# Gated attention with a low-rank mixer: order of loads around slot 7, PSUM tiles of the first pairs, whole-block squares in the first batch, cover in the short slots

## The chip, the cores and the metric

The kernel runs on one core of one Trainium2 chip. The metric is device microseconds of one execution, the median of several runs. The core has TensorE (PE) for matmuls, VectorE (DVE) and ScalarE (ACT) for elementwise work, GpSimd (POOL), and SyncE (SP), whose queue issues nearly all the DMA transfers of this kernel, one after the other.

## The reference

```python
def _attn_ref(u, v, z):                       # u, v: 8 x 3136 x 256, z: 8 x 3136 x 64
    scale = 1.0 / S
    scores = scale * np.matmul(z, z.transpose(0, 2, 1))
    attn = np.maximum(scores, 0.0) ** 2
    return u * np.matmul(attn, v)

def _moe_ref(x, U, V, w_ch1, w_ch2):          # U: 3136 x 32, V: 32 x 3136, w: 256 x 1024, 1024 x 256
    h = x.transpose(0, 2, 1) @ U @ V
    u = x + h.transpose(0, 2, 1)
    ch = np.maximum(u @ w_ch1, 0.0) @ w_ch2
    return u + ch
```

For each of eight batches: scores of z with itself, a squared relu, the product with v, a gate by u (this gives x), a rank-32 mix along the sequence (this gives x + h), and a two-layer channel mix with a residual. Inputs and output are float32; the kernel works in bfloat16 inside.

## The kernel before

**Tiling.** The 3136 rows of a batch are cut into NG = 7 groups: six of 512 rows (g = 0 to 5) and a short one of 64 rows (g = 6, called NQ). The scores are symmetric, so a block of 512 x 512 scores is computed once (two pairs of matmuls, 1024 columns each) and turned by a transposing DMA for its mirror image (`issue_turn`, line 416). Blocks are bfloat16 tiles `blk0` to `blk19`; scores and all other matmul results pass through four PSUM tiles `ps0` to `ps3` (`take_ps`, line 148). A block on the diagonal is made in a split layout (`score_finish_split`), with a turn of its own, the split turn. The product of scores and v is called AV.

**From score to block.** `rectify` (line 366) turns the PSUM result of a pair into bfloat16 by a relu on ACT or DVE, and `square` (line 362) squares it in place on DVE: line 364 in the profile. `score_finish` (line 491) does this for each pair on its own, so that each half of a block (1024 columns) has its own square, held until the planner thinks that its relu is done. In slot 0 the first pairs are handled by a list, `ways`: the first two, called "half", are split between ACT (lines 376, 380) and DVE (lines 377, 381), each engine taking one of the two 512-column banks of the same PSUM tile.

**Slots.** The work goes through 56 slots, t = 0 to 55, one for each item (b, g), in the loop from line 1347. Slot t holds the AV of item t; from t = 7 on x + h of item t - 7 (`u2_unit`, line 823: the rank-32 part, the sum, and the transposing DMA that gives the tile u2T, line 785); and from t = 8 on the channel mix of item t - 8 (`ch1_part`, line 922, which reads u2T and w1, then `ch2_stream`, line 1010, which reads w2). The score pairs of later items, `todo[t]`, are laid in between as cover: PE has them to do while other work waits. The slots with g = 6 (t = 6, 13, 20, ...) are the short ones: the AV of 64 rows is `av_small` (line 703, 50 matmuls), and the order of the parts is the list `order` (line 1439). The scores of the short group are turned by a DMA into `last_sb` (`last_turn`, line 551).

**What sets the order.** The schedule is written out by the program (`manual_schedule`). A planner clock (`clock[0]`) advances by the matmuls that are issued, in units of 256 columns, and `book` keeps estimated times for ACT, DVE and SP. `hold(due, f)` (line 121) puts work off until the planner clock reaches `due`; `emit` (line 1110) merges a stream of AV matmuls with queues of other parts, each with its place in the stream. On the chip each engine runs its instructions in the order in which they were issued, and waits by semaphore.

**First loads.** In the first slots weights are loaded between other work: `first_loads` (line 1232) gives U in slot 2, V in slots 3 and 4, w1 in slot 5 and w2 in slot 6 (`load_w`, line 1183, two halves). In slots 0 to 7 each load step is held at `clock + 5 + 22 * i` (line 1379), and the next group's u (`load_u`, line 304) at `clock + 60` (line 1381). In slot 7 (batch 1, g = 0) the z of the next batch is loaded in two pieces, the second with small transfers for the tail rows of z and v. Casts of what a slot loaded are held in the next slot (line 1365). In slot 7 x + h is done for the first time, and slot 8 holds the first channel mix.

Of the kernel before, what the change touches and what calls it, by code (L numbers as in the profile page):

```python
# [18 lines left out]
def kernel(  # L19
# [11 lines left out]
    nc = tc.nc  # L31
# [70 lines left out]
    ready_turns = []  # L102
    urgent = []
    slot = [0]
    ways = ["half", "half", "both", "dve"]
    waiting = [0]

    def needed(e):
# [12 lines left out]
    def hold(due, f):  # L121
        held.append((due, len(held), f))
# [243 lines left out]
    def rectify(dst, src, b, part=1, whole=False):  # L366

        ready = clock[0] + 3
        dve, act = max(free_at["dve"], ready), max(free_at["act"], ready)
        if whole and slot[0] == 0:  # L370
            dve += 6.5 * waiting[0]
            ends = {"dve": dve + DVE, "act": act + 19, "both": max(act + 8.7, dve) + 7.5}
            given = bool(ways)
            way = ways.pop(0) if ways else min(ends, key=lambda w: ends[w])
            if way == "half":
                nc.scalar.activation(out=dst[:, 0], in_=src[:, 0], func=AF.Relu, scale=scale)
                nc.vector.tensor_scalar(  # L377
                    out=dst[:, 1], in0=src[:, 1], scalar1=scale, scalar2=0.0, op0=ALU.mult, op1=ALU.max
                )
                nc.scalar.activation(out=dst[:, 0], in_=dst[:, 0], func=AF.Square)  # L380
                nc.vector.tensor_tensor(out=dst[:, 1], in0=dst[:, 1], in1=dst[:, 1], op=ALU.mult)  # L381
                done = max(book("act", ready, 5.2), book("dve", ready, 6.2))
                return done, max(book("act", ready, 5.2), book("dve", ready, 3.5))
            if way == "dve":
                if not given:
                    run_held(ready + 9)
                return one_pass(dst, src, ready)
            if way == "act":
                nc.scalar.activation(out=dst, in_=src, func=AF.Relu, scale=scale)
                nc.scalar.activation(out=dst, in_=dst, func=AF.Square)  # L390
                done = book("act", ready, 8.7)
                book("act", ready, 8.7)
                return done, free_at["act"]
        elif dve + 8 * part < act:
            nc.vector.tensor_scalar(  # L395
                out=dst, in0=src, scalar1=scale, scalar2=0.0, op0=ALU.mult, op1=ALU.max
            )
            return book("dve", ready, 11.2 if part == 1 else 6.4), None
        nc.scalar.activation(out=dst, in_=src, func=AF.Relu, scale=scale)  # L399
        return book("act", ready, 8.7 if part == 1 else 5.3), None  # L400
# [36 lines left out]
    def score_pairs(jobs):  # L437
# [50 lines left out]
            )  # L488
        return made

    def score_finish(made):
        for dst, k, ps, turn, key in made:
            if key and split(*key):
                score_finish_split(dst, k, ps, turn, key)
                continue
            if turn:
                J, g, b = turn
                unturned[blocks[b, g, J][0]] = False
            done, whole = rectify(dst, ps, key[0] if key else 0, whole=True)
            ps_free[k] = done  # L500
            waiting[0] += whole is None

            def finish(dst=dst, turn=turn, key=key, whole=whole):
                if whole is None:
                    waiting[0] -= 1
                    square(dst)
                if key:
                    squared[key] = squared.get(key, 0) + 1
                if turn:
                    hold(clock[0] + (7 if whole is None else 1), lambda: ready_turns.append(turn))  # L510

            hold(whole or done, finish)

    def score_finish_split(flat, k, ps, h, key):
# [23 lines left out]
    def score_burst(jobs):  # L538
        score_finish(score_pairs(jobs))


    def place_of(jt):

# [662 lines left out]
    def load_V(i0):  # L1206
# [27 lines left out]
        3: lambda: load_V(0),  # L1234
        4: lambda: load_V(2),
        5: lambda: load_w(0),
        6: lambda: load_w(1),
    }


# [70 lines left out]
    clock[0] = 43  # L1311
    free_at.update(dve=46, act=47)
    jobs0 = jobs_of(0, 0)
    score_burst(jobs0[:1])
    score_burst(jobs0[1:2])
    score_burst(jobs0[2:3])
    clock[0] = 60

# [1 line left out]
    for b in range(B):  # L1320
        for g in range(NQ):
            t = b * NG + g - 1
            new = jobs_of(b, g)
            if g == 0 and b > 0:
                x, y = (5, 10) if b == 1 else (5, 11)
                todo[t - 2] += new[:x]
                todo[t - 1] += new[x:y]
                todo[t] += new[y:12] if b == 1 else new[y:]
                todo[t + 1] += new[12:] if b == 1 else []
            elif b == 0 and g == 0:  # L1330
                todo[0] += new[3:]
            elif b == 0 and g and g % 2 == 0:
                todo[t] += new[:-1]
                todo[t + 1] += new[-1:]
            else:
                todo[t] += new
# [5 lines left out]
    direct = (B - 1, 0)  # L1342

    def early(b, g):
        return b > 1 and g == NQ

    for t in range(n_items):
        slot[0] = t
# [9 lines left out]
            load_u(*items[t + 1])  # L1358
        if t > NG and g_now == NQ and b_next < B:
            hold(clock[0] + 60 + 70, lambda b=b_next: load_u(b, NQ))  # L1360
        if t == n_items - 3:
            xTs[direct] = take_block()[1][:, : GT // 2, :].rearrange("p a (q d c) -> p (a q) d c", d=ND, c=P)
            x_turn(*direct, xTs[direct])
        for i, f in enumerate(casts_next):
            hold(clock[0] + (90 if g_now == NQ and b_next > 1 else 60 if t == NG else 15 if t >= NQ else 45) + 12 * i, f)
        casts_next = []
        spare += spare_next
        spare_next.clear()
        steps = load_part(b_next, g_now) if b_next < B else []
        steps += first_loads[t]() if t in first_loads else []  # L1370

        def load(step):
            casts_next.extend(step())
# [1 line left out]
        for i, f in enumerate(steps):  # L1375
            if t > NG:
                load(f)
            else:
                hold(clock[0] + 5 + 22 * i, lambda f=f: load(f))
        if t <= NG:  # L1380
            hold(clock[0] + 60, lambda t=t: load_u(*items[t + 1]))
        if g_now == 0 and t:
            last_turn(att[0])
        if b_next < B and g_now == 2:
# [24 lines left out]
        if av and full:  # L1409

            last = nA - 9
            for h, x, y in zip(hs, (4, 22, 36, 62), (16, 32, 48, last)):
                qc.append((x, 1, False, one(h, 0)))
                qc.append((y, 0 if y == 32 else 1, y != 32, lambda h=h, y=y: (scores(y != 32), one(h, 1)())))
            n = len(mine) - 3
            qs += [(9 + 74 * i / n, 1, False, lambda: scores(1)) for i in range(n)]
        elif av:

            if mix:
                qc += [(x, 1 - way, False, lambda way=way: ch1_small(*mix, way, box1)) for way, x in ((0, 36), (1, 48))]  # L1420
            if fin:
                qc.append((72, 2, False, lambda: (ch2_small(*fin), av_small(att[0], NQ))))
            k = min(2, len(mine) // 3)
            n = len(mine) - 3 * k
            at = [1 + 80 * i / n for i in range(n)]
            if t == 0:
                at, k = [16, 30, 46, 50, 64, 68, 78, 84, 92], 0
                qs += [(4, 0, True, lambda: scores(1)), (12, 0, True, lambda: z_turn(0, 2 * GT, on_act))]
                qs += [(x, 0, True, lambda: scores(1)) for x in (24, 40, 56, 72, 88)]
                qm.append((20, 0, False, lambda: (cast_z(2, 0, on_dve), cast_z(2, 1, on_dve), book("dve", 0, 8))))  # L1430
                qm.append((34, 0, False, lambda: z_turn(0, 4 * GT, on_act)))
                qm.append((58, 0, False, cast_tail))
                qm.append((62, 0, False, lambda: z_turn(0, 6 * GT, on_act)))
            qs += [(x, 1, False, lambda: scores(1)) for x in at]
            qs += [(x, k, True, lambda: scores(k)) for x in (16, 48, nA - 2) if k]
        else:

            small = (lambda: None) if early(*att) else (lambda: av_small(*att))
            order = mine[:1] + [small] + mine[1:]
            if mix:  # L1440
                c0, c1, d0, d1, c2, c3, d2, d3 = parts(mix, box1)
                up = [lambda: u2_unit(*u2i)]
                if fin:
                    late = mine[-1:] if early(*att) else []
                    rest = mine[: len(mine) - len(late)]
                    order = [c0] + rest[:1] + [c1, d0, d1] + [c2] + rest[1:] + [c3, d2, d3] + up
                else:
                    order = up + [small, c0, c1, d0, d1, c2, c3, lambda: t1_all(att[0]), d2, d3]
            qc += [(0, 0, False, f) for f in order]
# [81 lines left out]
```

## Time and profile before

| what | us |
|---|---|
| median of 3 runs | 982.09 (981.95 to 982.22) |
| the profiled execution | 986.39 |
| its span | 984.6 |
| PE busy in the span | 973.7 |
| DVE busy | 628.2 |
| ACT busy | 482.4 |
| POOL busy | 15.2 |

The span runs from the first to the last instruction that the profiler recorded; the execution's own time holds a little more around it. All times of instructions below are in microseconds from the start of this span, on the one core. PE's busy time counts matmuls alone; loading of weights runs beside them. A line such as `L364 DVE` names the line of the program and the engine. `[0.85 <-DVE blk L364]` behind a row says that the engine was idle for 0.85 us before it, and what released it. `SPq` is the transfer queue that SP fills. `x_bf` is the bfloat16 x or x + h, `u2T` its transpose, `zzT` the transposed z, `stage` a float32 landing place for loads. In a row of the timeline, `x8` counts the instructions that were drawn together. Matmuls come in pairs on the two halves of the rows, shown as `64*128`.

### The profile page before, as it was taken

The numbers are of one execution on the slowest core, as the hardware profiler recorded it, in microseconds if no ns is written. First come the engines' busy times: TensorE is split into PE (matmuls) and PEld (weight loads), VectorE is DVE, ScalarE is ACT, GpSimd is POOL, SyncE is SP. The second block draws the span as 40 slices with busy tenths as digits, with TensorE's granted clock in tenths as the row PEclk, the third lists the DMA queues.
The fourth block names the chain that finished last, engine by engine and source line by source line (L and its number), as shares of the span: only waits on it lengthen the run. The fifth ranks groups of instructions, "written<-read, shape, count | busy, mean of one in ns | idle before, by whom it ended". The sixth has DMA issues, their size and how long they took to land.

```text
span 984.6 us, 35373 instructions
## 1 busy us (share of the span) xinstructions
PE 973.7 (99%) x16163; PEld 773.4 (79%) x16163; DVE 628.2 (64%) x811; ACT 482.4 (49%) x565; POOL 15.2 (2%) x25
## 2 busy tenths in 40 slices
PE   8999899999999999999999999999999999999998
PEld 5788677877778778787777877788777887778766
DVE  6878755668556685566755667556775567653363
ACT  7877642456324473355633555334654346431353
POOL 4200000000000000000000000000000000000000
PEclk9999999999999999999999999999999999999999
DMA  8899999979997799987999879997799978965153
GB/s 269 193 225 192 228 196 188 223 153 197 195 204 167 160 192 192 205 170 170 185 208 207 154 178 179 223 189 153 173 207 206 194 144 163 186 135 95 55 114 99
DMA packets 372405, 176.37 MB, mean 179 GB/s; under 512 B 347296, under 2 KB 350624, under 8 KB 372256
## 3 DMA queue, kind: packets, MB, share of 16 engines
q1 hardware_dynamic: 372256, 174.12, 85.6%
q8 instruction: 126, 2.06, 0.9%
q14 instruction: 23, 0.19, 0.1%
HBM read 62.56 MB, written 25.69 MB: 90 GB/s over the span
## 4 chain that ended last, share of the span: by engine, by line
PE 96%; DVE 1%; ACT 1%; DMA 1%; issue 0%; DVEq 0%
PE ps L184 93%; PE ps L714 1%; DMA u2T<-x_bf 1%; PE ps L797 1%; ACT blk L399 0%; PE ps L1096 0%; DVE blk L364 0%; PE ps L1300 0%; PE ps L331 0%; DVE blk L377 0%; DVE blk L381 0%; DVE x_bf L749 0%; DVE blk L406 0%; DVE out_sb L870 0%; DVE blk L395 0%
## 5 line engine op out<-in xcount | busy, mean ns | idle before, releaser
L184 PEld LDWEIGHTS <-blk 64*128 64x128 bf16 x12288 | 609.7, 94 | 159.9 <-POOLq L174 9.6
L184 PE MATMUL ps<-v_bf,blk 64*128 64x256 bf16 x9216 | 613.0, 269 | 2.3 <-DVE blk L364 1.1
L399 ACT ACTIVATE blk<-ps 128x1024 bf16<-128x1024 f32 (+1 forms) x335 | 315.3, 970 | 346.6 <-PE ps L184 343.2
L364 DVE TENSOR_TENSOR blk<-blk 128x1024 bf16<-128x1024 bf16 x350 | 221.1, 656 | 49.1 <-ACT blk L399 48.4
L184 PE MATMUL ps<-u2T,w_bf 64*128 64x512 bf16 (+1 forms) x1792 | 227.9, 350 | 2.8 <-DMA u2T<-x_bf 2.8
L184 PE MATMUL ps<-w_bf,blk 64*128 64x256 bf16 x3072 | 192.0, 269 | 0.0
L959 DVE TENSOR_SCALAR blk<-ps 128x1024 bf16<-128x1024 f32 x105 | 128.5, 1224 | 97.6 <-PE ps L184 96.6
L962 ACT ACTIVATE blk<-ps 128x1024 bf16<-128x1024 f32 x87 | 88.3, 1022 | 119.0 <-PE ps L184 118.8
L184 PE MATMUL ps<-zzT 64*128 64x512 bf16 (+2 forms) x902 | 129.8, 327 | 0.6 <-ACT zzT L340 0.6
L184 PEld LDWEIGHTS <-w_bf 64*128 64x128 bf16 x1792 | 84.3, 94 | 30.2 <-POOLq L174 5.0
L749 DVE TENSOR_TENSOR x_bf<-ps,u_sb 128x1024 bf16<-128x1024 f32 x48 | 58.7, 1222 | 71.4 <-PE ps L184 71.4
L870 DVE TENSOR_TENSOR out_sb<-ps,x_bf 128x1024 f32<-128x1024 f32 x42 | 51.4, 1224 | 58.1 <-PE ps L184 58.1
L1082 DVE TENSOR_TENSOR out_sb<-ps,out_sb 128x1024 f32<-128x1024 f32 x42 | 51.4, 1224 | 18.6 <-PE ps L184 18.3
L184 PEld LDWEIGHTS <-zzT 64*128 64x128 bf16 x902 | 41.2, 94 | 6.9 <-ACT zzT L340 1.5
L184 PE MATMUL ps<-t_sb,V_bf 64*128 64x256 bf16 x200 | 20.6, 269 | 0.0
L395 DVE TENSOR_SCALAR blk<-ps 128x1024 bf16<-128x1024 f32 (+1 forms) x14 | 16.6, 1185 | 5.9 <-PE ps L184 5.1
L206 DVE CAST v_bf<-stage 128x1024 bf16<-128x1024 f32 (+1 forms) x30 | 18.5, 617 | 0.0
L184 PE MATMUL ps<-v_bf,last_sb 64*128 64x256 bf16 x192 | 18.5, 269 | 0.0
L204 ACT CAST v_bf<-stage 128x1024 bf16<-128x1024 f32 (+1 forms) x18 | 18.1, 1005 | 0.0
L206 DVE CAST x_bf<-out_sb 128x1024 bf16<-128x1024 f32 x22 | 15.2, 689 | 0.3
L1082 DVE TENSOR_TENSOR blk<-ps,blk 128x1024 f32<-128x1024 f32 x5 | 6.1, 1225 | 11.9 <-PE ps L184 11.8
L204 ACT CAST x_bf<-out_sb 128x1024 bf16<-128x1024 f32 x13 | 13.5, 1037 | 0.0
(83 smaller groups left out, 239.1 us busy)
## 6 DMA issues: line engine op xcount, KB each, us to landing
u_sb<-in_u_dram SPq DMA_DIRECT2D x48, 512.0 KB, 5.1
stage<-in_v_dram SPq DMA_DIRECT2D x42, 512.0 KB, 6.1
out_dram<-out_sb SPq DMA_DIRECT2D x42, 512.0 KB, 3.1
stage<-in_z_dram SPq DMA_DIRECT2D x7, 512.0 KB, 5.9
blk<-in_v_dram SPq DMA_DIRECT2D x5, 512.0 KB, 6.3
out_dram<-blk SPq DMA_DIRECT2D x5, 512.0 KB, 2.6
blk<-blk SPq DMA_TRANSPOSE x156, 5.1
blk<-in_moe_w_ch_dram SPq DMA_DIRECT2D x4, 512.0 KB, 4.9
```

Source lines behind the costliest of these rows:

```text
L184: ins = nc.tensor.matmul(**args)
L204: nc.scalar.copy(out=out, in_=in_)
L206: nc.vector.tensor_copy(out=out, in_=in_)
L364: nc.vector.tensor_tensor(out=a, in0=a, in1=a, op=ALU.mult)
L395: nc.vector.tensor_scalar(out=dst, in0=src, scalar1=scale, scalar2=0.0, op0=ALU.mult, op1=ALU.max)
L399: nc.scalar.activation(out=dst, in_=src, func=AF.Relu, scale=scale)
L714: nc.tensor.matmul(out=ps[c * hp : c * hp + rows, h, :D], lhsT=smalls[b][h * hp : (h + 1) * hp, place_of(jt), :], rhs=v_bfs[b][h * hp : (h ...
L749: nc.vector.tensor_tensor(out=xs[b, g][:rows, :n, :], in0=four(box["ps"])[:rows, :n, :], in1=u_sbs[b, g][:rows, :n, :], op=ALU.mult,)
L870: nc.vector.tensor_tensor(out=o[:rows, :n, :], in0=four(ps)[:rows, :n, :], in1=x, op=ALU.add)
L959: nc.vector.tensor_single_scalar(out=r, in_=ps[:, :, :gw], scalar=0.0, op=ALU.max)
L962: nc.scalar.activation(out=r, in_=ps[:, :, :gw], func=AF.Relu)
L1082: nc.vector.tensor_tensor(out=o, in0=acc, in1=o, op=ALU.add)
```

## The change

- Loads: w2 is loaded in slot 7 (`NG` in `first_loads`) instead of slot 6, ahead of the z pieces in the list of steps; the steps of slot 7 are held at `clock + 78 + 12 * i` instead of `clock + 5 + 22 * i`. The u for slot 7's item is loaded at `clock + 5` in slot 6 instead of `clock + 60`, and in slot 7 the next group's u at `clock + 88`. The small u of batch 1 is loaded at the start of slot 7. The casts of slot 7's loads are held at `clock + 45` instead of `clock + 60` of slot 8.
- `av_small` of batch 1 is laid at place 64 of slot 7's stream; `early` now holds for b > 0, so that slot 13 no longer holds it.
- The first two score pairs of slot 0 go through the new `shared_pairs`: ACT's halves of both pairs lie in one PSUM tile and DVE's halves in another. The "half" way in `rectify` is gone.
- In slots 1 to 5 a block of batch 0 whose first pair is made there (and which is not a split one) is squared as a whole, 2048 columns in one instruction, once both relus are done (`merged`, `whole_block`). Its turn becomes ready 7 units after the square instead of 7 or 1.
- In the short slots x + h (`up`) comes first, then the parts of the mix, then score pairs; two pairs (`late`) instead of one are kept for the middle of the second layer. From batch 2 on the slot ahead of a short one has four score pairs of the next batch's first group instead of six, and the short one has three instead of one.

```diff
-    ways = ["half", "half", "both", "dve"]
+    ways = ["both", "dve"]
...
+    def whole_block(n, key, turn):
+        waiting[0] -= 1
+        if n == 2:
+            square(blocks[key][1], 11.7)
+            squared[key] = 2
+        if turn:
+            hold(clock[0] + 7, lambda: ready_turns.append(turn))
...
+            if key and not key[0]:
+                n = halves[key] = halves.get(key, 0) + 1
+                if n == 1 and 0 < slot[0] < NQ:
+                    merged.add(key)
+                if key in merged:
+                    finish = lambda n=n, key=key, turn=turn: whole_block(n, key, turn)
             hold(whole or done, finish)
...
+    def shared_pairs(jobs):
+        (ka, a), (kb, d) = take_ps(), take_ps()
+        for i, (b, g, (J, h)) in enumerate(jobs):
...
+            for jj in range(2):
+                key = J * GT + 2 * h + jj
+                nc.tensor.matmul(
+                    out=(a if jj == i else d)[:, jj, :],
...
+            dst = blocks[b, g, J][1][:, 2 * h : 2 * h + 2, :]
+            x, y = dst[:, i], dst[:, 1 - i]
+            nc.scalar.activation(out=x, in_=a[:, i], func=AF.Relu, scale=scale)
+            nc.vector.tensor_scalar(out=y, in0=d[:, 1 - i], scalar1=scale, scalar2=0.0, op0=ALU.mult, op1=ALU.max)
+            nc.scalar.activation(out=x, in_=x, func=AF.Square)
+            nc.vector.tensor_tensor(out=y, in0=y, in1=y, op=ALU.mult)
...
-        6: lambda: load_w(1),
+        NG: lambda: load_w(1),
...
-    score_burst(jobs0[:1])
-    score_burst(jobs0[1:2])
+    shared_pairs(jobs0[:2])
...
-                x, y = (5, 10) if b == 1 else (5, 11)
+                x, y = (5, 10) if b == 1 else (5, 9)
...
     def early(b, g):
-        return b > 1 and g == NQ
+        return b > 0 and g == NQ
...
+        if t == NG:
+            hold(clock[0] + 2, lambda: load_u(1, NQ))
...
-            hold(clock[0] + (90 if g_now == NQ and b_next > 1 else 60 if t == NG else 15 if t >= NQ else 45) + 12 * i, f)
+            hold(clock[0] + (90 if g_now == NQ and b_next > 1 else 45 if t == NG + 1 else 15 if t >= NQ else 45) + 12 * i, f)
...
-        steps += first_loads[t]() if t in first_loads else []
+        steps = (first_loads[t]() if t in first_loads else []) + steps
...
-                hold(clock[0] + 5 + 22 * i, lambda f=f: load(f))
+                hold(clock[0] + (78 + 12 * i if t == NG else 5 + 22 * i), lambda f=f: load(f))
         if t <= NG:
-            hold(clock[0] + 60, lambda t=t: load_u(*items[t + 1]))
+            hold(clock[0] + (5 if t == NQ else 88 if t == NG else 60), lambda t=t: load_u(*items[t + 1]))
...
+            if t == NG:
+                qc.append((64, 2, False, lambda: av_small(1, NQ)))
...
-                    late = mine[-1:] if early(*att) else []
+                    late = mine[-2:] if early(*att) else []
                     rest = mine[: len(mine) - len(late)]
-                    order = [c0] + rest[:1] + [c1, d0, d1] + [c2] + rest[1:] + [c3, d2, d3] + up
+                    order = up + [c0, c1, d0, d1, c2, c3, d2, d3] + rest
```

More of the change, by code (lines that the diff above doesn't have):

```diff
@@ L374, in rectify @@
             way = ways.pop(0) if ways else min(ends, key=lambda w: ends[w])
[L375 to L383, printed above, removed]
             if way == "dve":
@@ L489, in score_pairs @@
         return made
+    halves, merged = {}, set()
+    def whole_block(n, key, turn):
[5 more added lines that the diff above has]
+            hold(clock[0] + 7, lambda: ready_turns.append(turn))
     def score_finish(made):
@@ L539, in score_burst, with finish @@
         score_finish(score_pairs(jobs))
+    def shared_pairs(jobs):
+        (ka, a), (kb, d) = take_ps(), take_ps()
+        for i, (b, g, (J, h)) in enumerate(jobs):
+            zzT = zzTs[b]
+            if h == 0:
+                blocks[b, g, J] = take_block()
+            for jj in range(2):
+                key = J * GT + 2 * h + jj
+                nc.tensor.matmul(
+                    out=(a if jj == i else d)[:, jj, :],
+                    lhsT=half(zzT, jj, key * P, P),
+                    rhs=half(zzT, jj, groups[g][0], GW),
+                    start=True,
+                    stop=True,
+                )
+            pe(GW / 256)
+            dst = blocks[b, g, J][1][:, 2 * h : 2 * h + 2, :]
[4 more added lines that the diff above has]
+            nc.vector.tensor_tensor(out=y, in0=y, in1=y, op=ALU.mult)
+            ps_free[ka] = book("act", clock[0] + 3, 5.2)
+            ps_free[kb] = book("dve", clock[0] + 3, 6.2)
+            book("act", 0, 5.2)
+            book("dve", 0, 3.5)
+            def finish(key=(b, g, J)):
+                squared[key] = squared.get(key, 0) + 1
+            hold(max(free_at["act"], free_at["dve"]), finish)
     def place_of(jt):
```

## The prediction

> **What bounds the kernel now.** I read the page first, then what the matmul engine waited for, the chain that ended last, and tables and timelines of the three places where that chain leaves the engine.
>
> ```profile
> span 984.6 us, 35373 instructions
> PE 973.7 (99%) x16163; PEld 773.4 (79%) x16163; DVE 628.2 (64%) x811; ACT 482.4 (49%) x565; POOL 15.2 (2%) x25
> ```
>
> PE is the bound: 99% busy, every other engine far below. The number of matmuls is the same in both kernels, so the change can only move PE's idle time, its clock and the two ends. PE's waits name all the idle time to be had:
>
> ```profile
> PE ps L184 <- DMA u2T<-x_bf: 2.8, 1, 2.8
> PE ps L184 <- DVE blk L364: 1.1, 2, 0.8
> PE ps L184 <- ACT blk L380: 0.8, 1, 0.8
> PE ps L184 <- ACT zzT L340: 0.6, 1, 0.6
> ```
>
> With the smaller ones they sum to 6.5 us; one wait, for the first x + h's turn, is almost half. The chain shows how it hangs, and that nothing follows it but PE:
>
> ```profile
> 102.97 8.44 DMA u2T<-x_bf
> 111.41 0.05 issue
> 111.45 87.65 PE ps L184 x1396
> ```
>
> The turn took 8.44 us; the median of its tile is 3.6. The table by microsecond (length, busy time, matmuls, granted clock, DMA share, GB/s) shows a second price, a halved clock after the idle time:
>
> ```profile
> 111.00:112.00 1.00, 0.55 (x4) 0.56 1.22 260
> 112.00:113.00 1.00, 1.00 (x12) 0.50 1.30 259
> 113.00:114.00 1.00, 1.00 (x12) 0.50 1.05 235
> 114.00:115.00 1.00, 1.00 (x16) 0.73 0.76 107
> ```
>
> Idle 2.76, and 0.55 x 0.5 + 0.50 + 0.50 + 0.27 = 1.55 lost to the clock: 4.3 us for the whole stall.
>
> **Part 1, slot 7's loads.** SP issues every transfer in order, and these were ahead of the turn:
>
> ```profile
> 100.94 1.09 SPq L308 DMA_DIRECT2D u_sb<-in_u_dram  x2
> 102.97 2.25 SPq L785 DMA_TRANSPOSE u2T<-x_bf  x1
> ```
>
> Also two w2 halves and two z pieces, from 95.04 to 100.39. After the change SP sees, ahead of the turn, only u of the first group (moved to slot 6), the turn of the short scores, the small u and a split turn; w2, z, z2, two u and v come behind it. What makes its input, x + h at 102.94, does not move, so by 3.6 (median) to 5.7 (midway to 8.4) it lands at 106.6 to 108.7. PE wants it later than before: the short slot's AV (50 matmuls, 1.56 us in the chain at 92.46) moves from slot 13 into slot 7, so 108.65 becomes some 110.1. The margin is 1.4 to 3.5 us and the stall goes whole: -4.3 against the profiled execution. The moved AV costs nothing in sum; slot 13 loses what slot 7 gains.
>
> What of it the timed runs have is unsure. The profiled execution took 986.39 (984.6 span, 1.79 around it), the median is 982.09: 4.30 less. Its matmuls are the same, so I spread the 4.30 over what can vary: idle 6.5, slow clock 1.55, and 4.3 from the last matmul (about 980.3) to the end, together 12.35. The stall's 4.3 are 35%, so 1.5 of the difference, and 2.8 remain in timed runs. Bounds: 0 (the whole difference is the stall) and 4.3 (none of it is).
>
> Next in line in slot 8: w2 and z are now cast there, and z's four small tail transfers stand at SP behind two block turns. I place their issue at 113 to 119 and landing at 118.5 to 122.5; DVE and ACT reach the casts that want them at about 120.5 to 121.4, and wait in order. Queued behind on ACT and DVE are the relus of the mix's hidden tiles, whose PSUM tiles PE wants next. 0 to 1.5 us; I take 0.4, since half the landing interval is past the need and PE has other work for some 0.5 us. If hidden, 0.
>
> **Part 2, head.** The first pairs shared PSUM tiles between ACT and DVE:
>
> ```profile
> 6.13 0.69 DVE L377 TENSOR_SCALAR blk<-ps 128x512 bf16<-128x512 f32 x1 [2.29 <-ACT blk L376]
> 8.00 0.86 DVE L381 TENSOR_TENSOR blk<-blk 128x512 bf16<-128x512 bf16 x1
> ```
>
> DVE waited for ACT's relu (5.50 to 6.10), though its scores were done near 5.5. With a tile for each engine DVE starts 0.6 earlier. Against that, matmuls three and four now wait for the first two relus, and the pair behind them with it: issue moves to about 6.45, ending 6.85, against AV's start at 6.81, so nothing is lost. Of the 0.6, ACT's transposed z at 9.90 (0.6 of PE waits) takes part: the wait for L381 on the way to it is only 0.25, and PE's next one for DVE 0.21. I take 0.4; bounds 0.6 gained and 0.3 lost.
>
> **Part 3, whole-block squares** (the first batch's, slots 1 to 5). Two squares of 1024 become one of 2048. From this row and those of 512 (0.42) and 1024 (0.68) I estimate 1.22 for it:
>
> ```profile
> 88.91 0.99 DVE L364 TENSOR_TENSOR attn_small<-attn_small 128x1600 bf16<-128x1600 bf16 x1 [0.32 <-ACT attn_small L604]
> ```
>
> So 0.14 less DVE work for a block, worth 0 at 64% busy. But a square now waits for both relus, and in slot 1 that is tight:
>
> ```profile
> 27.45 0.28 PE L184 MATMUL ps<-v_bf,blk 64*128 64x256 bf16 x2 [0.85 <-DVE blk L364]
> 28.00 4.77 ACT L399 ACTIVATE blk<-ps 128x1024 bf16<-128x1024 f32 x5 [0.98 <-PE ps L184]
> 29.05 1.25 DVE L364 TENSOR_TENSOR blk<-blk 128x1024 bf16<-128x1024 bf16 x1 [1.05 <-ACT blk L399]
> ```
>
> PE's order there: one score pair (27.57), six AV matmuls, then two AV matmuls of the next block, at 28.1. Before, they wanted only the square of its first half, done at 27.99 (two squares from 26.71, 1.28 in all). Now they want the whole square, which wants the relu of the pair just scored: 28.00 to 29.02 on ACT, then 1.22 on DVE, 30.27, PE at 30.32. New wait 2.2 us, and the score pairs queued behind on PE, which feed ACT, are late by as much. Bounds 1.7 (ACT's and DVE's durations at their shortest, 0.9 and 0.95) and 3.5 (DVE at 1.25 per 1024, as in the third row, where POOL casts from 28.72). I take 2.2: POOL's cast stands behind later matmuls. The next whole block is squared behind a relu of DVE: 0.4 (0 to 1.0). Later slots score further ahead: 0.
>
> [...]
>
> **Part 4, short slots.** x + h goes first, three score pairs instead of one follow the mix, and the slot before has four instead of six. PE never idles there in the trace (87.65 us without a break, above), so 0 gained; what is lost if a PSUM tile comes late is a relu's part, 0 to 0.3 in six slots, 1.8.
>
> **Sum.** Timed: 982.09 - 2.8 - 0.4 + 2.2 + 0.4 + 0.4 = 981.9. Against the profiled execution: 986.39 - 4.3 - 0.4 + 2.2 + 0.8 = 984.7.
>
> **Rivals.** *The stall is as dear in timed runs, and slot 8 is quiet*: -4.3 - 0.4 + 2.2 + 0.4 = 980.0; with the shorter wait (1.7) and nothing after it, 979.1. For it: 2.76 idle is a queue's order, the same in every run; against it: the 4.30 us between profile and median. Case value 979.5.
>
> *Slower, by the clock in slot 1*: 2.2 idle is near the 2.76 after which the clock was 0.5 for 3 us; if it falls, as at 111 to 115, 1.55 more, and ACT's late relus let it fall deeper: 981.9 + 1.55 = 983.5, and with a wait of 3.5, 984.8. It is slower by 0.2% from an idle time of some 2.8 with the fall. For it: that row; against it: 0.85 idle at 27.45 left no mark. [...]
>
> *Slower, slot 8 stalls in the first one's place*: z's tails come 3 us late instead of 0.4, and the clock halves: 981.9 + 2.6 + 1.55 = 986.0; it decides from 2.6 us of stall with its clock. For it: DMA share 1.05 to 1.30 at 111 to 114, with w2, z and u now in it; against it: 0.76 at 114.
>
> *Nothing is changed in the stall*: the turn is late still, because a split turn precedes it: 982.09 - 0.4 + 3.0 = 984.7.
>
> **How the numbers follow.** A measurement of this kernel tells about 0.2%, 1.96 us, from no change: 980.13 to 984.05. Even trade, 981.9 (its own range 980.2 to 984.0): 0.37. Dear stall, 979.5: 0.32. Clock in slot 1: 0.16, slot 8: 0.08, late turn: 0.07, together 0.31. Faster 0.32, same 0.37, slower 0.31. The range leaves out one in ten below, 978.9, and above, 985.2.
>
> **What would show it.** Part 1: no wait of PE for u2T, and a turn of some 4 us at 103. Part 2: DVE's first relu at 5.5. Part 3: a wait of 2.2 for DVE L364 near 28. Slot 8: waits below 0.5 near 121. Wrong if slot 1 shows no wait, if PE idles in short slots, or if the profiled gain is not the timed one.

## The result, and the profile after

The changed kernel took 983.74 us (median of 14 executions, 982.90 to 986.66) against 982.24 for the kernel before (14 executions, 981.69 to 983.35). The ratio, estimated from all executions of both and so not quite that of the medians, is 1.0019, 95% interval 1.0010 to 1.0028: slower by 1.0 to 2.8 us, at the edge of the 0.2% that I had called telling. Forecast was 981.9; the range, 978.9 to 985.2, holds the time, but the direction is wrong. The profiled execution took 986.04, its span 984.3, less than the 986.39 and 984.6 of before: by single profiles the change gains a little, by medians it loses. That contradiction is what had to be explained.

The page and PE's waits of the changed kernel (us in total, times, longest):

```profile
span 984.3 us, 35342 instructions
PE 974.4 (99%) x16163; PEld 783.5 (80%) x16163; DVE 632.5 (64%) x795; ACT 480.6 (49%) x562; POOL 13.7 (1%) x25
```

```profile
PE ps L184 <- DVE blk L364: 3.1, 3, 2.1
PE ps L1340 <- DVE blank L70: 1.0, 1, 1.0
PE ps L558 <- DVE blk L569: 0.8, 1, 0.8
PE ps L184 <- ACT zzT L340: 0.6, 1, 0.6
```

The wait for the turn of x + h is gone, and a wait of 2.1 for a square is there instead. The chain that ended last shows it in slot 1, and that from slot 7 on PE runs through (start, us, what):

```profile
28.30 0.52 PE ps L184 x4
28.82 0.02 issue
28.84 1.03 ACT blk L390
29.88 0.02 issue
29.90 1.24 DVE blk L364
31.14 0.05 issue
31.18 3.19 PE ps L184 x19
...
110.64 90.02 PE ps L184 x1466
```

This is the forecast sequence: score pair, relu, one square of 2048 columns, PE. Behind it, the table by microsecond (length, busy time, matmuls, granted clock, DMA share, GB/s) shows the clock falling:

```profile
30.00:31.00 1.00, 0.00 (x0) 0.90 0.88 332
31.00:32.00 1.00, 0.82 (x6) 0.50 0.73 299
32.00:33.00 1.00, 1.00 (x12) 0.50 0.12 41
33.00:34.00 1.00, 1.00 (x12) 0.50 0.00 0
34.00:35.00 1.00, 1.00 (x18) 0.89 0.00 0
```

That is 0.82 x 0.5 + 0.50 + 0.50 + 0.11 = 1.5 us. So in these two executions the kernel before paid 4.3 in slot 7, and the changed one paid 2.05 + 1.5 in slot 1 and, as it turned out, 0.85 in the head: PE reaches the first wait of slot 1 at 28.30 instead of 27.45.

The first turn of x + h, in the transfer queue of the changed kernel and where PE first reads it:

```profile
107.52 1.75 SPq L825 DMA_TRANSPOSE u2T<-x_bf  x1
...
114.73 0.59 PE L184 MATMUL ps<-u2T,w_bf 64*128 64x512 bf16 x4
```

It landed at 110.58, after 3.1 us instead of 8.44, with 4.15 us to spare.

### The profile page after: what moved, and what is told of

It is laid out like the page before. It is cut to its first block, busy times and chain, and to the rows that moved or that the text cites. A ratio compares the mean times of both kernels' runs of the same rounds, so it can differ in the third digit from the quotient of the medians.

```text
span 984.3 us, 35342 instructions
## 1 busy us (share of the span) xinstructions
PE 974.4 (99%) x16163; PEld 783.5 (80%) x16163; DVE 632.5 (64%) x795; ACT 480.6 (49%) x562; POOL 13.7 (1%) x25
## 4 chain that ended last, share of the span: by engine, by line
PE 98%; DVE 1%; ACT 1%; issue 0%; DVEq 0%
PE ps L184 95%; PE ps L754 1%; PE ps L837 1%; PE ps L1136 0%; ACT blk L390 0%; DVE blk L364 0%; PE ps L1340 0%; PE ps L331 0%; DVE x_bf L789 0%; PE ps L558 0%; ACT last_sb L390 0%; ACT zzT L340 0%; DVE blk L569 0%; DVE blk L775 0%; DVE blk L1108 0%
## 5 line engine op out<-in xcount | busy, mean ns | idle before, releaser
L364 DVE TENSOR_TENSOR blk<-blk 128x1024 bf16<-128x1024 bf16 (+2 forms) x331 | 219.2, 682 | 46.3 <-ACT blk L390 44.8
L999 DVE TENSOR_SCALAR blk<-ps 128x1024 bf16<-128x1024 f32 x111 | 135.9, 1224 | 104.8 <-PE ps L184 104.0
L1002 ACT ACTIVATE blk<-ps 128x1024 bf16<-128x1024 f32 x81 | 82.2, 1022 | 124.4 <-PE ps L184 120.5
L184 PEld LDWEIGHTS <-w_bf 64*128 64x128 bf16 x1792 | 88.7, 94 | 23.3 <-POOLq L174 5.2
L386 DVE TENSOR_SCALAR blk<-ps 128x1024 bf16<-128x1024 f32 x16 | 19.6, 1224 | 9.2 <-PE ps L184 8.5
L204 ACT CAST x_bf<-out_sb 128x1024 bf16<-128x1024 f32 x19 | 19.7, 1037 | 0.0
L204 ACT CAST v_bf<-stage 128x1024 bf16<-128x1024 f32 x15 | 15.6, 1040 | 0.0
L754 PE MATMUL ps<-v_bf,attn_small 64*64 64x256 bf16 x400 | 13.1, 270 | 0.0
```

The costliest lines, as they stand in the source:

```text
L184: ins = nc.tensor.matmul(**args)
L204: nc.scalar.copy(out=out, in_=in_)
L364: nc.vector.tensor_tensor(out=a, in0=a, in1=a, op=ALU.mult)
L386: nc.vector.tensor_scalar(out=dst, in0=src, scalar1=scale, scalar2=0.0, op0=ALU.mult, op1=ALU.max)
L754: nc.tensor.matmul(out=ps[c * hp : c * hp + rows, h, :D], lhsT=smalls[b][h * hp : (h + 1) * hp, place_of(jt), :], rhs=v_bfs[b][h * hp : (h ...
L999: nc.vector.tensor_single_scalar(out=r, in_=ps[:, :, :gw], scalar=0.0, op=ALU.max)
```

## The experiments

Each was timed beside the kernel before on the same chip. That kernel's median came out at 983.25 in the first four, 982.97 in the next four, 983.18 in the third four and 982.27 in the last two, so ratios are compared. Where a ratio and the two medians tell different sizes, both are given.

**e1_again: the kernel before, a second profile.** No edit.

> The kernel before, unchanged, profiled a second time and timed beside itself. Theory P (the wait for the first turn of x + h is a matter of one profiled execution, and the timed runs hardly have it): the turn at 103 us lands within some 4 to 6 us this time, PE waits less than 1 us for it, the profiled time is within 1.5 us of the median, 982.2. Theory Q (the wait is the queue's order and the same in every run; the changed kernel gains 4.3 us there and loses them elsewhere): the turn takes some 8.4 us again, PE waits 2.8 us, clock 0.5 after it, profiled 986.4. The ratio to the kernel before is 1.000 by both.

983.02 us against 983.25, ratio 1.000 (0.9989 to 1.0010); profiled 983.61. PE's wait for u2T and the table around it:

```profile
PE ps L184 <- DMA u2T<-x_bf: 1.4, 1, 1.4
```

```profile
108.00:109.00 1.00, 0.69 (x14) 1.00 0.16 36
109.00:110.00 1.00, 0.00 (x0) 1.00 1.30 288
110.00:111.00 1.00, 0.89 (x14) 1.00 0.84 154
```

Half the wait, and the clock stays at 1.00. The turn took 7.1 us, more than theory P said, but the price is 1.4 and not 4.3. Three more experiments that left slot 7 alone show waits of 1.1, 1.1 and 0.7 (e3, e4, e7), none with a fall of the clock there: in e7 it read 1.00 at 109 to 113, and in e3 and e4, as in e1, the 1396 matmuls behind the wait took 86.16 us, against 87.65 in the profile with the fall. The profile that I forecast from had the dearest of five. Neither theory's figures came: the wait was above the 1 us of P and half of Q's 2.8.

**e2_loads: part 1 alone.**

```diff
-        6: lambda: load_w(1),
+        NG: lambda: load_w(1),
...
-                hold(clock[0] + 5 + 22 * i, lambda f=f: load(f))
+                hold(clock[0] + (78 + 12 * i if t == NG else 5 + 22 * i), lambda f=f: load(f))
...
+                qc.append((64, 2, False, lambda: av_small(1, NQ)))
```

and the other lines of the diff on loads and `early`.

> The kernel before with part 1 alone: order of loads in slots 6 to 8 and the AV of batch 1's short group in slot 7. Theory P: the trace shows no wait for u2T, and the timed median is 981.2 to 982.4 (0 to -1.0). Theory Q: 977.9 to 979.4 (-4.3 to -2.8). Either way PE shows no new idle time over 0.5 us in slots 7 and 8.

982.49 against 983.25, ratio 0.9987 (0.9976 to 0.9998): about -1.3 us by the ratio, between the theories' figures and nearer to P, and -0.8 by medians, inside P. No wait for u2T. The turn:

```profile
103.32 2.16 SPq L785 DMA_TRANSPOSE u2T<-x_bf  x1
```

It landed at 106.86 and PE wanted it at 110.53. Part 1 does what it says; there was at most about a third of 4.3 to be had.

**e3_merge: whole-block squares alone**, with `merged` and `whole_block` as in the change.

```diff
+            if key and not key[0]:
+                n = halves[key] = halves.get(key, 0) + 1
+                if n == 1 and 0 < slot[0] < NQ:
+                    merged.add(key)
+                if key in merged:
+                    finish = lambda n=n, key=key, turn=turn: whole_block(n, key, turn)
             hold(whole or done, finish)
```

> The kernel before with the whole-block squares alone. By the trace of the changed kernel: a wait of 2.05 us for DVE L364 near 30 us (here near 29, the head is as before) and, in some executions, 1.5 us from a halved clock behind it. If that is the whole cost: 982.2 + 2.1 = 984.3 in runs without the fall of the clock, 985.9 in those with it. Rival (the time lost in slot 1 is taken back by the end of slot 5, since DVE has less to do): within 0.5 us of the kernel before.

986.42 against 983.25, ratio 1.0035 (1.0021 to 1.0048): 2.1 to 4.7 us slower. Nothing is taken back. PE's row in slot 1:

```profile
30.73 0.40 PE L184 MATMUL ps<-v_bf,blk 64*128 64x256 bf16 x2 [2.05 <-DVE blk L364]
```

The granted clock of the whole span was 1.000 in five of ten executions (985.4 to 985.9) and 0.996 to 0.998 in the other five (986.9 to 989.8).

**e4_shared: two PSUM tiles alone.**

```diff
-    score_burst(jobs0[:1])
-    score_burst(jobs0[1:2])
+    shared_pairs(jobs0[:2])
```

> The kernel before with the two PSUM tiles of the first pairs alone. Theory H (the third and fourth matmul wait for the first two relus, and matmuls of one row half issued one by one run no longer side by side): PE reaches slot 1 some 0.85 us later than before (28.30 against 27.45 us in the changed kernel), the median is +0.85, 983.1. Rival (what the head loses, slot 0's cover takes back by the end): 982.2, within 0.3. The forecast had it at -0.4.

982.63 against 983.25, ratio 0.9997 (0.9985 to 1.0010), which holds both no change and the forecast's -0.4. Theory H falls: PE reached slot 1's first wait at 26.84, earlier than the 27.45 of before. The head of e4, then of the changed kernel; the matmul shapes are the same:

```profile
5.96 0.39 PE L542 MATMUL ps<-zzT 64*128 64x512 bf16 x2 [0.81 <-DVE blk L553]
6.17 0.39 PE L184 MATMUL ps<-zzT 64*128 64x512 bf16 x2
6.55 0.61 PE L184 MATMUL ps<-v_bf,blk 64*128 64x256 bf16 x8
```

```profile
6.34 0.61 PE L558 MATMUL ps<-zzT 64*128 64x512 bf16 x2 [0.81 <-DVE blk L569]
6.72 0.66 PE L184 MATMUL ps<-zzT 64*128 64x512 bf16 x2
7.14 1.08 PE L184 MATMUL ps<-v_bf,blk 64*128 64x256 bf16 x8
```

The order is right and DVE's relu is early (5.21 and 5.60 instead of 6.13), but in the changed kernel's profile the matmuls ran at about half speed until 10.3 us, in e4 at full speed from 4.3. I read that from their durations, such as 1.08 against 0.61 for eight AV matmuls: the granted clock in the tables is 1.00 in both.

**e5_after_again: the changed kernel, a second profile.** No edit.

> The changed kernel once more: what of its first trace is the same in every execution. Theory S (the wait for the whole square is order and comes each time; the halved clock behind it and the slow clock in the head are a matter of the execution): again 2.05 us for DVE L364 near 30 us and no wait for u2T; the clock of 0.5 at 31 to 34 us and the matmuls at half speed up to 10.3 us may be missing, and then the profiled time is 983.3 and not 986.0. Timed: two groups again, near 983.3 and near 986. Rival: both are the same each time, and all is at 986.

984.14 against 982.97, ratio 1.0016 (1.0005 to 1.0027); profiled 984.08. Theory S holds:

```profile
29.49 0.28 PE L184 MATMUL ps<-v_bf,blk 64*128 64x256 bf16 x2 [2.05 <-DVE blk L364]
...
127.87 0.61 PE L184 MATMUL ps<-w_bf,blk 64*128 64x256 bf16 x8 [0.34 <-DVE blk L999]
```

```profile
30.00:31.00 1.00, 1.00 (x18) 1.00 0.43 172
31.00:32.00 1.00, 1.00 (x18) 1.00 0.08 25
```

Again 2.05 to the hundredth, and no fall of the clock behind it. Of the 12 executions seven took 983.0 to 984.2 at a clock of 0.999 or 1.000, five 985.3 to 987.0 at 0.997 or 0.998; of the 14 above, nine and five. Where a clock fell can be seen in profiled executions alone; for the others the clock of the whole span stands in. The second row is slot 8's new wait, 0.34, where I had put 0.4. It came as forecast, though at 127 and not near 121: DVE stood 2.13 us for z's tail until 124.52, and the mix's relu (L999) behind it was late. The first turn of x + h is not waited for; a later one is, 0.44 us at 189.10.

**e6_merge_late and e9_late_again: whole-block squares from slot 2 on.**

```diff
-                if n == 1 and 0 < slot[0] < NQ:
+                if n == 1 and 1 < slot[0] < NQ:
```

> The changed kernel with whole-block squares from slot 2 on instead of slot 1. Theory S (all of the loss is the wait in slot 1): no wait over 0.5 us for DVE L364 other than the 0.85 at some 27 us that the kernel before has too, no fall of the clock in slot 1, median 981.0 to 982.0, as without any whole-block squares. Rival (whole squares cost turns and PSUM tiles in slots 2 to 5 too): between this and the changed kernel, 982.5 to 983.5.

> The changed kernel with whole-block squares from slot 2 on, a second time, as the base of the next three. 981.6 again (981.0 to 982.0), 1.4 us below the kernel before.

981.57 against 982.97, ratio 0.9987 (0.9979 to 0.9996), and 981.25 against 983.18, ratio 0.9981 (0.9971 to 0.9991). Only the old wait is left in slot 1 (e6):

```profile
27.12 0.28 PE L184 MATMUL ps<-v_bf,blk 64*128 64x256 bf16 x2 [0.85 <-DVE blk L364]
```

One condition away from the changed kernel, this beats both kernels: no execution of 23 was above 982.8. Slot 1's squares cost some 2.8 us (1.0016 for e5 against 0.9987 for e6, timed together), which is more than the whole loss. e9 is the base of the next experiments.

**e8_no_merge: no whole-block squares.**

```diff
-                if n == 1 and 0 < slot[0] < NQ:
+                if n == 1 and False:
```

> The changed kernel without whole-block squares. By the single runs so far (loads -0.8, two tiles -0.6, squares +3.2 against the kernel before): -1.4, 981.0 to 982.0, if the parts add and the short slots are worth 0; at least 1.5 us below the changed kernel. Rival (the parts do not add, since the turn's wait took up what came late before it): within 0.5 of the kernel before.

981.94, ratio 0.9985 (0.9977 to 0.9994), the same as e6 within the intervals: what remains of whole squares, in slots 2 to 5, is worth nothing that these runs can tell. The other parts together are a gain, 0.6 to 2.3 us by this interval, where the forecast had 2.8 for them.

**e7_short and e10_late_no_short: the short slots' part, alone and taken out of e6.**

```diff
-                    order = [c0] + rest[:1] + [c1, d0, d1] + [c2] + rest[1:] + [c3, d2, d3] + up
+                    order = up + [c0, c1, d0, d1, c2, c3, d2, d3] + rest
```

with (5, 9) for (5, 11) and two `late` pairs; e10 undoes all three.

> The kernel before with the short slots' order and the split of score pairs alone. By the forecast 0, bounds 0 to +1.8: 982.2 to 983.3, within 0.5 of the kernel before of the same call, and no new wait of PE after 120 us. Rival (x + h first in the short slots gives more time to its turn or less cover to the mix): a wait of PE over 0.3 us in each of six short slots, +1.8.

> The same as the base, with the short slots' order and the split of score pairs as they were before the change. Theory N (part 4 is worth nothing, its +0.7 in the run alone is scatter): within 0.4 us of the base, 981.2 to 982.0. Rival (part 4 costs what its run alone showed): 0.7 to 0.9 us below the base, 980.8.

Alone: 983.67 against 982.97, ratio 1.0009 (0.9998 to 1.0020). Taken out: 982.20 where the base, timed beside it, has 981.25, ratios 0.9992 (0.9984 to 1.0001) against 0.9981 (0.9971 to 0.9991). So part 4 looks like a loss of 0.7 in the one and a gain of 1.0 in the other. The loss is inside its interval. The gain is clearer than the two ratios tell: nine of the base's eleven executions lie below the lowest of e10 (981.56), so neither theory N nor its rival fits. PE's waits after 130 us are two in e7, 0.26 and 0.24 at 208 us, and none over 0.15 in e10 or in its base, so no wait of PE shows where a gain of 1.0 comes from. What part 4 is worth is not settled.

**e11_late_no_shared: the old head in e6.**

```diff
-    shared_pairs(jobs0[:2])
+    score_burst(jobs0[:1])
+    score_burst(jobs0[1:2])
```

> The same as the base, with the first two pairs in one PSUM tile each as before the change. If two tiles gain what the run alone showed, 0.3 to 0.6: 982.0 to 982.2. Rival (the slow clock in the head takes the gain back on average): within 0.2 of the base, with fewer runs above 982.3.

981.62 against the base's 981.25, ratios 0.9984 and 0.9981: 0.3 in favour of two tiles, which the intervals don't tell from nothing.

**e12_but_first: one block excepted.**

```diff
-                    merged.add(key)
+                    (merged if first else first).add(key)
```

> The changed kernel with one block excepted from the whole-block squares, the first one of slot 1, which PE waited for; all others of slot 1 stay whole. Theory S1 (that one wait is all the loss): no wait of 2.05 us, as fast as the base, 981.2 to 982.0, and not one run above 985. Rival (all whole squares of slot 1 cost): a new wait of 0.5 to 1.5 us for the next block, 982.5 to 983.2.

982.50, ratio 0.9992 (0.9983 to 1.0001): between the base and the changed kernel, and nothing above 984. The wait moves on to the next block, smaller:

```profile
33.35 0.72 PE L184 MATMUL ps<-v_bf,blk 64*128 64x256 bf16 x10 [0.53 <-DVE blk L364]
```

The eleven lie 1.25 us above the base by medians. So the first block's wait is most of the loss and not all, as the rival had it: for the first two blocks of slot 1 the scores are made too shortly ahead of their use for a whole square.

**e13_head_filled: seven matmuls of zeros in the head's gap** (in e6), which replace no work.

```diff
+            if i:
+                filler(7)
```

> The changed kernel with whole-block squares from slot 2 on (981.6 and 981.3 in two calls), and seven matmuls of zeros in PE's gap between the first and the second pair. Theory G (the gap of 0.8 us decides when the clock is granted): matmuls at full speed from 7 us at the latest in the trace, the first wait of slot 1 at 27.2 us or earlier, median 981.0 to 981.4 and no run above 982.0. Rival (it is not the gap but the phase of the execution): no change, 981.3 to 981.6, runs up to 982.5.

981.18 against 982.27, ratio 0.9986 (0.9977 to 0.9995), as e6. The profile had full speed from 4.3 us, but reached slot 1's wait only at 28.24, for another cause: PE waited 0.9 for a hand-over through POOL's queue and 0.6 for z's cast, which came later than in e6. One run at 982.44 goes against theory G. Whether the gap decides the head's clock stays open.

**e14_slot1_filled: thirty matmuls of zeros in slot 1's wait** (in the changed kernel), which replace no work.

```diff
+            if len(bursts) == 2:
+                filler(30)
```

> The changed kernel with thirty matmuls of zeros in slot 1, ahead of the matmuls that wait for the whole square: some 1.7 us of the 2.05 us are then busy, the rest is idle. Theory C (PE's idleness there is what lets the clock fall): clock 1.0 throughout 28 to 36 us, the upper group of times is gone, all runs within 982.9 to 984.3, median 983.2. Rival (the clock falls for another reason, or the upper group comes from elsewhere): runs near 986 in about two of five still, median 983.7 or more.

983.14 against 982.27, ratio 1.0006 (0.9996 to 1.0015). The filling, what is left of the wait, and the clock:

```profile
28.64 1.85 PE L560 MATMUL ps<-blank 128*128 128x128 bf16 x30
...
31.09 0.28 PE L184 MATMUL ps<-v_bf,blk 64*128 64x256 bf16 x2 [0.17 <-DVE blk L364]
```

```profile
30.00:31.00 1.00, 0.92 (x15) 1.00 0.83 234
31.00:32.00 1.00, 0.92 (x14) 1.00 0.90 369
32.00:33.00 1.00, 1.00 (x22) 1.00 0.28 107
```

PE gets on at 31.09, as late as ever (31.18 in the changed kernel from the same start of 28.2 to 28.3), but the group near 986 is gone: all eleven executions at 0.999 or 1.000, none above 985.02, the median as theory C had it (the spread, 982.33 to 985.02, is wider than it said). The changed kernel itself was not timed beside these; at its rate so far, 10 executions of 26, none in eleven would have a chance of about 0.5%. So theory C holds as far as these runs can tell: PE's idleness is what lets the clock fall there, and useless matmuls kept it up.

## Why the prediction was wrong

**Part 1, the step that failed: "The stall's 4.3 are 35%, so 1.5 of the difference, and 2.8 remain in timed runs."** I spread the 4.30 us between profile and median evenly over all that could vary. In fact most of it, about 3 us, was this stall: the four other profiles with the old order of loads (e1, e3, e4, e7) wait 0.7 to 1.4 us there, not 4.3, and keep their clock. What could be gained was 1.3 by the ratio (0.2 to 2.4, e2) and 0.8 by medians, so the term was mis-sized by some 1.5 to 2 us. A dear execution is rare: of the 121 of the kernel before that stand beside the experiments, 8 took 985.7 to 986.4 at a clock of 0.997 or 0.998, as the profiled one did, and of the 80 of e2, e6, e8, e9, e10, e11 and e13, with the new order of loads and no whole square in slot 1, none took more than 984.5. That the eight lost their time in this stall is likely, but they have no trace. I should have stood nearer to the lower bound (the whole difference is the stall): 8.44 us was the longest landing of its tile, the profile was 0.4% above the median, and only that stall, of all that the profile shows, had two prices, the wait and the clock, that can go together. The mechanism itself held: in the eleven profiles with the new order the turn lands in 3.1 to 3.6 us, with about 4 us to spare.

**Part 3: right, with a rival's price on top.** The new wait was put at 2.2 and measured 2.05 in each of three profiles. The next block's 0.4 was 0.17. The square of 2048 columns took 1.23, the estimate 1.22; POOL's cast began only behind it (31.91 in the changed kernel, where the square ended at 31.13), so the 3.5 for a cast beside it was not put to the test. The fall of the clock, which I had as a rival with 0.16, happened, by the clock of the whole span, in 5 of 14 and 5 of 12 executions of the changed kernel: as a mean, 0.4 x 1.5 = 0.6 us that the sum lacked. It should have been a term with a chance, not another case. The same 2.05 us of idle time had a granted clock of 0.50 behind it in two traces (the changed kernel's first, where 0.70 of 28 to 29 us was busy, and e3, where 0.67 was) and 1.00 in a third (e5); what decides between them the runs don't show. That this rival's 983.5 lies near the measured 983.74 is luck: the nine executions without the fall have a median of 983.33, so the kernel is slower by about 1.1 us even there.

**Part 2: the mechanism right, the size not to be told.** In the six profiles of kernels with one tile for each pair (the kernel before twice, e2, e3, e7, e11) slot 1's first wait ends at 27.34 to 27.85, mean 27.57. In nine with two tiles and no filling of the head (the changed kernel twice, e4, e6, e8, e9, e10, e12, e14) it ends at 26.50 to 28.30, mean 27.43. The forecast gain of 0.4 is 0.14 here, because in four of the nine (the changed kernel's first, e8, e12, e14) the matmuls stay at about half speed until some 10 us, in the others only until 4 to 6; with one tile it is always near 7. DVE's first relu does start earlier, as forecast (5.21 in e4 and 5.60 in the changed kernel, 6.13 before); what decides the speed stays open.

**Slot 8** was put at 0.4; of eleven profiles with the new order of loads six show 0.27 to 0.34 and five nothing. The stall there, a rival at 0.08, did not come. But the second turn of x + h now lands 0.3 to 1.2 us before its use, where it had 6 us before: nearly the next wait. **Part 4** was put at 0, and the runs disagree on it (+0.7 alone, -1.0 in e6).

The sum with what was measured: -1.3 (loads) - 0.1 (head) + 2.05 + 0.17 (squares) + 0.6 (clock, as a mean) + 0.17 (slot 8, as a mean) = +1.6, against +1.5 by medians and +1.9 by the ratio. The first term is known to 1 us and part 4 is left out, so that they meet this closely is luck in part. The group near 986 lies 2.7 above the lower one, of which the clock in slot 1 is 1.5; the rest isn't explained. The one traced execution of that group also had the slow head (28.30 against 26.61 in e5).

## What to carry to other kernels

One profile is one draw: where its time stands well above the median, look for the stall that can vary (a transfer with the longest landing of its kind, a clock that fell) and price that stall from several profiles before building on it. The joined square waited for the later of its two relus (it started at 29.90 in the changed kernel, that relu ended at 29.87): before joining two halves, look whether anyone waits for the first of them, most of all early, where work is made just ahead of its use. Idle time of the matmul engine had a second price here, 1.5 us of slow clock behind 2.05 us of it in the changed kernel's first profile and none in e5; as a chance, such a price belongs in the sum. With thirty useless matmuls in that place (e14) the granted clock stayed at 1.00.

## What the runs showed of the hardware

I had not expected that behind the same 2.05 us of idle time, after 0.85 us shortly before, the granted clock stands at 0.50 for some 3 us in some executions (traced in the changed kernel and in e3) and at 1.00 in others (traced in e5): by the clock of the whole span, it fell in 10 of 26 executions of the changed kernel. Behind idle times of 1.4, 1.1, 1.1 and 0.7 in slot 7 it did not fall in their four profiles. By the durations of the matmuls (0.39 us for a pair of score matmuls where they are fast, 0.61 to 0.66 where they are slow), the time at which they first ran at full speed varied between 4, 6 and 10 us over executions of the same two-tile head; slot 1's first wait ended at 26.50 to 28.30 there. The granted clock of the tables reads 1.00 there all the same, so for that stretch I went by the durations. A square of 2048 columns in bfloat16 took 1.23 us on DVE, two of 1024 columns 1.28 (at 26.71 in the kernel before), so joining them saved DVE next to nothing here.
